# First channel layer of a mixer: product banks copied to SBUF by ScalarE instead of being added from PSUM by VectorE

## The chip, the cores and the metric

The kernel runs on one core of one Trainium2 chip. A core has five engines that work side by side, each with a queue of its own: TensorE (PE in the profile; its weight loads are PEld), VectorE (DVE), ScalarE (ACT), GpSimd (POOL) and SyncE (SP), which here only issues transfers. The metric is the device time of one execution in microseconds (us), as the median of several runs.

## The reference

Eight batches of attention with 12 heads, 448 tokens and head size 64, followed by an MLP mixer over 768 channels (token layer 448-256-448, channel layer 768-1536-768), all in float32:

```python
q_n, k_n = rmsnorm(q, g_q), rmsnorm(k, g_k)
attn = softmax(q_n @ k_n.T / 8)
x = (attn @ v) as (batch, 448, 768)
u = x + (relu(x.T @ w_tok1) @ w_tok2).T
out = u + relu(u @ w_ch1) @ w_ch2
```

## The kernel before

**Stages.** Batch b's mixing runs while the attention of batch b + 1 is computed; the last batch has no attention beside it. Batches 0 and 1 multiply the two channel layers plainly. In batches 2 to 7 both layers use a scheme with fewer products: a layer's operands are taken as blocks, 15 products (`NF9`) of sums of blocks are formed, and the results are sums of products. The sums of the weights, the "forms", are made once by POOL in batches 0 to 2 (`form`, L295), in the tiles of `raw_pool` (5 buffers), and stored in DRAM (`ws1`, `ws2`); they are placed every `FORMS_EVERY` us of a nominal clock. The sums of the data are made by VectorE and POOL as they are needed (`X1_STEPS` for layer one, in the tile `tu`; `X_STEPS` for layer two, in the slots of `hb`).

**Items.** `ch1(b, f, o)` is product f of layer one, half o of its columns; `ch2(b, f, x)` is product f of layer two, half x. Each such item is four float32 matmuls of 128x128 by 128x224 (eight records in the trace), 1.51 us of TensorE, so that a batch has 30 items of ch1 and then 30 of ch2, numbered here from 0 to 59; (4,1) means f = 4, second half.

**PSUM.** There are eight banks: four in the pool S of the attention's scores (`s_ps`, `d_ps`), two in the pool O of its values, two in the pool M (`m_ps`). A product of ch1 with o = 0, and every second product of ch2, takes a bank of S (then named `c_ps`); the others take one of M. A bank is free again when the operations that read it are done. In `ch1`, the table `C1_STEPS` says what reads it: "a" is a ScalarE copy (L989), "v" a VectorE sum and "g" a POOL sum (both L992); "P" is the bank, (m, n) a block of the hidden layer, A, B, C running sums. So most of the products are added by VectorE straight out of PSUM, 128x448 at a time, once for each o. ReLU is applied by ScalarE to a whole block (L996) when its last sum is made; `put_off` postpones this, and the data's sums, to the start of the next item.

**Attention between the items.** A pair step of attention is cut into two blocks. The first one (`first_block`) has two scores, the last values of the pair before, `row_sums` and a third score; the second one (`second_block`) has four scores and four values. `place` puts six blocks of 5.5 to 7.5 us ahead of the items 0, 9, 16, 25, 33 and 40 (`BLOCKS`): second, first, second, first, second, first. What goes with a block is issued right after it (`beside`) or spread over the items up to the next block (`between`). With a first block come, for the next pair: two squares on ScalarE (L1374, the first ahead of the block's last item, the second within the block), two sums of squares ("reduce", VectorE, L1388), then `fold` (four small ScalarE copies "half", L1396), `guess` (two small VectorE operations), three `newton` steps (POOL, four small operations each, L1418 to L1421), the sums of exponentials `group_sums` ("es", VectorE, L482, 128x896), and the denominators of the pair before (dt, rc, rd, uT on VectorE, L543 to L560). With a second block come two scales (VectorE, L403, which need the newtons), four transposes (VectorE, L418), two multiplications by g (ScalarE, L421) and four es sums. The exponentials themselves (L445) are on ScalarE.

**Order.** The order on TensorE, VectorE, ScalarE and POOL is the order in which the program issues the instructions; no scheduler moves them. An engine works through its queue in this order, and an instruction that waits holds up all that is behind it.

The lines that decide where a sum of squares stands:

```python
ahead, beside = (squares[:1], squares[3:]) if t > BIG else ([], [])
between = [item(group_sums, t, k) for k in (1, 2) if live]
...
between += roots[:1] + ends[:2] + roots[1:2]
```

`squares` is square, reduce, square, reduce for the two halves of a pair; `squares[3:]` is the second reduce, and `roots[:1]` is `fold`.

## Time and profile before

| | |
|---|---|
| median of 3 runs | 1316.96 us (1314.82 to 1317.05) |
| profiled execution | 1318.08 us, of which the span from first to last instruction is 1316.2 us |
| mean granted TensorE clock | 0.992 of full speed |
| batch 2 (mixing) begins | 426.7 us; batches 3 to 7 at 587.9, 741.7, 895.3, 1048.7 and 1196.5 us |
| VectorE sum, 128x448, one operand in PSUM (L992) | 0.61 us |
| VectorE sum, 128x896, all in SBUF (L1021, L482) | 1.08 us at its shortest, 1.17 in the mean |
| POOL sum, 128x448 (L992) and 128x896 (L1021) | 1.14 us at its shortest, and 2.09 us |
| ScalarE copy of a bank (L989), ReLU of a block (L996) | 0.53 and 0.95 us |

A span of the trace is read in three ways here: which engine waited for which, in sums; the instructions of one engine in order of time, with the idle time ahead of each and what ended it; and busy time and granted clock by stretches.

### The profile page before, as it was taken

The numbers are of one execution on the slowest core, as the hardware profiler recorded it, in microseconds if no ns is written. First come the engines' busy times: TensorE is split into PE (matmuls) and PEld (weight loads), VectorE is DVE, ScalarE is ACT, GpSimd is POOL, SyncE is SP. The second block draws the span as 40 slices with busy tenths as digits, with TensorE's granted clock in tenths as the row PEclk, the third lists the DMA queues.
The fourth block names the chain that finished last, engine by engine and source line by source line (L and its number), as shares of the span: only waits on it lengthen the run. The fifth ranks groups of instructions, "written<-read, shape, count | busy, mean of one in ns | idle before, by whom it ended". The sixth has DMA issues, their size and how long they took to land.

```text
span 1316.2 us, 19628 instructions
## 1 busy us (share of the span) xinstructions
PE 1262.6 (96%) x7048; PEld 871.8 (66%) x7048; DVE 835.9 (64%) x1280; ACT 403.5 (31%) x775; POOL 469.0 (36%) x727
## 2 busy tenths in 40 slices
PE   5999999999999997999999999999999999999996
PEld 3444444444445675696777777786876967797996
DVE  6998769654463566755768368765677557664343
ACT  6663433123320243402443044321434024300210
POOL 1300100079975785430343203450234303430242
PEclk9999999999999999999999999999999999999998
DMA  9666456898888977596567766495765965476664
GB/s 210 172 178 162 120 139 169 203 259 236 234 202 230 212 210 183 114 247 123 115 174 157 191 144 148 115 232 139 167 153 113 252 122 129 122 183 157 177 178 82
DMA packets 480272, 225.60 MB, mean 171 GB/s; under 512 B 375204, under 2 KB 441764, under 8 KB 480164
## 3 DMA queue, kind: packets, MB, share of 16 engines
q1 hardware_dynamic: 462690, 206.68, 65.2%
q0 software_dynamic: 4480, 15.73, 3.9%
q10 hardware_dynamic: 12994, 1.84, 0.9%
q8 instruction: 58, 0.95, 0.3%
q14 instruction: 50, 0.41, 0.1%
HBM read 178.36 MB, written 45.81 MB: 170 GB/s over the span
## 4 chain that ended last, share of the span: by engine, by line
PE 77%; DVE 10%; DMA 4%; SPq 3%; POOL 2%; issue 2%; ACT 2%; DVEq 0%; ACTq 0%; POOLq 0%
PE m_ps L1047 12%; PE c_ps L1047 10%; PE s_ps L441 8%; PE c_ps L979 8%; PE m_ps L979 7%; PE o_ps L514 7%; PE m_ps L862 5%; PE m_ps L1010 4%; PE m_ps L935 4%; PE m_ps L1030 4%; PE t_ps L820 2%; PE m_ps L820 2%; DVE es L482 2%; DMA qk_t<-in_k_dram 2%; DVE hb L1021 1%
## 5 line engine op out<-in xcount | busy, mean ns | idle before, releaser
L445 ACT ACTIVATE e<-s_ps 128x448 f32<-128x448 f32 x294 | 141.4, 556 | 178.9 <-PE s_ps L441 168.9
L441 PE MATMUL s_ps<-qkT 64*64 64x448 f32 x1260 | 169.0, 547 | 2.5 <-DVE r L992 1.7
L1047 PE MATMUL m_ps<-hb,unit 128*128 128x224 f32 x768 | 160.4, 364 | 9.4 <-DVE r L992 9.4
L1047 PEld LDWEIGHTS m_ps<-hb,unit 128*128 128x128 f32 x768 | 150.3, 197 | 12.5 <-DVE r L992 11.1
L295 POOL TENSOR_TENSOR raw<-raw 128x128 f32<-128x128 f32 x256 | 135.2, 549 | 45.8 <-DMA out_dram<-turned 25.5
L514 PE MATMUL o_ps<-e,v 64*64 64x448 f32 x1148 | 144.8, 539 | 0.7 <-DVE uT L560 0.4
L1047 PE MATMUL c_ps<-hb,unit 128*128 128x224 f32 x672 | 135.8, 354 | 2.6 <-ACT e L445 2.0
L1047 PEld LDWEIGHTS c_ps<-hb,unit 128*128 128x128 f32 x672 | 126.3, 190 | 9.9 <-ACT e L445 4.3
L482 DVE TENSOR_TENSOR es<-es,e 128x896 f32<-128x896 f32 x90 | 105.7, 1175 | 14.6 <-ACT e L445 9.6
L441 PEld LDWEIGHTS s_ps<-qkT 64*64 64x64 f32 x1260 | 52.6, 132 | 84.1 <-issue 57.5
L979 PE MATMUL c_ps<-tu,unit 128*128 128x224 f32 x480 | 101.5, 354 | 3.9 <-ACT e L445 3.8
L979 PE MATMUL m_ps<-tu,unit 128*128 128x224 f32 x480 | 102.1, 356 | 1.7 <-DVE hb L992 1.7
L979 PEld LDWEIGHTS m_ps<-tu,unit 128*128 128x128 f32 x480 | 89.7, 190 | 9.9 <-issue 5.6
L979 PEld LDWEIGHTS c_ps<-tu,unit 128*128 128x128 f32 x480 | 90.1, 190 | 9.2 <-ACT e L445 7.6
L514 PEld LDWEIGHTS o_ps<-e,v 64*64 64x64 f32 x1148 | 52.7, 133 | 60.5 <-issue 48.0
L992 POOL TENSOR_TENSOR hb<-hb,r 128x448 f32<-128x448 f32 x36 | 49.5, 1401 | 117.6 <-DVE r L992 80.0
L1062 POOL TENSOR_TENSOR uT<-uT,r 128x448 f32<-128x448 f32 x42 | 52.5, 1262 | 104.0 <-DVE r L1062 92.0
L403 DVE TENSOR_TENSOR qk_t<-qk_t,rs 128x896 f32<-128x896 f32 (+1 forms) x42 | 55.6, 1361 | 43.5 <-POOL rs L1421 43.5
L961 POOL TENSOR_TENSOR tu<-uT 128x448 f32<-128x448 f32 x12 | 13.7, 1139 | 194.2 <-DVE uT L867 117.2
L862 PE MATMUL m_ps<-w_sb,h 128*128 128x448 f32 x192 | 74.4, 541 | 2.9 <-DVE uT L867 2.9
L1418 POOL TENSOR_TENSOR nt<-rs 128x56 f32<-128x56 f32 (+1 forms) x57 | 17.8, 313 | 160.2 <-DVE rs L1410 158.2
L1388 DVE TENSOR_REDUCE ms<-sq 128x28 f32<-128x896 f32 (+2 forms) x44 | 47.4, 1079 | 41.4 <-ACT sq L1374 38.3
(151 smaller groups left out, 1995.5 us busy)
## 6 DMA issues: line engine op xcount, KB each, us to landing
unit<-ws SPq DMA_DIRECT2D x240, 384.0 KB, 3.9
raw<-in_moe_w_ch_dram SPq DMA_DIRECT2D x72, 256.0 KB, 3.4
v<-in_v_dram SPq DMA_DIRECT2D x96, 112.0 KB, 3.9
xs<-xt SPq DMA_DIRECT2D x56, 168.0 KB, 4.5
out_dram<-turned SPq DMA_DIRECT2D x168, 56.0 KB, 2.0
unit<-wp SPq DMA_DIRECT2D x24, 384.0 KB, 4.7
ws<-raw POOLq DMA_DIRECT2D x16, 512.0 KB, 4.9
qk_t<-in_q_dram SPq DMA_DIRECT2D x144, 56.0 KB, 3.5
```

Of the source, the lines that this page charges most:

```text
L295: nc.gpsimd.tensor_tensor(out=at[o], in0=at[x], in1=at[y], op=ALU.add if op == "+" else ALU.subtract)
L403: nc.vector.tensor_tensor(out=x, in0=x, in1=r.unsqueeze(2).to_broadcast(list(x.shape)), op=ALU.mult)
L441: nc.tensor.matmul(out=pss[i][rows_of(i, a), 0:S], lhsT=qkT[h, 1, k * D:(k + 1) * D], rhs=qkT[h, 0, :], start=True, stop=True)
L445: nc.scalar.activation(out=e[:, i, :], in_=pss[i][:, 0:S], func=AF.Exp)
L482: nc.vector.tensor_tensor(out=es[:], in0=(es if k > 1 else st["e", t, 0])[:], in1=st["e", t, k][:], op=ALU.add)
L514: nc.tensor.matmul(out=st["o", p][a * D:(a + 1) * D, 0:S], lhsT=vt[rows, k * D:(k + 1) * D], rhs=e[rows, :], **kw)
L820: nc.tensor.matmul(out=st["t1", h][jc][:, 0:HC], lhsT=w1_sb[:, c, jc * P:(jc + 1) * P], rhs=st["x", b, h][:, :, c, :], start=start and c = ...
L862: nc.tensor.matmul(out=ps[:, 0:S], lhsT=st["h1", jc][:, cc * P:(cc + 1) * P], rhs=w2_sb[:, jc].rearrange("p c r -> p (c r)"), start=(jc == ...
L935: nc.tensor.matmul(out=ps, lhsT=a[:, o + 2 * half, :], rhs=natural(half * KF + t) if wide else u[:, half * KC + t, :], start=(t == 0 and h ...
L979: nc.tensor.matmul(out=ps[:, t * HS:(t + 1) * HS], lhsT=st["w"][:, tile_at % 6, :], rhs=x[:, k, :], start=(k == 0), stop=(k == 1))
L1010: nc.tensor.matmul(out=ps, lhsT=w[:, 3 * o + t, :], rhs=u[:, half * KC + t, :], start=(half == 0 and t == 0), stop=(half == 1 and t == KC ...
L1047: nc.tensor.matmul(out=ps[:, x * HS:(x + 1) * HS], lhsT=st["w"][:, tile_at % 6, :], rhs=hb[:, X_SLOT[f], i, :], start=(i == 0), stop=(i == 3))
```

## The change

In layer one every bank is copied by ScalarE, to a block of `hb` (`C1_COPY`) or to a tile T of `raw_pool`, one for both halves; the sums are made after the second half, 128x896 at a time, between SBUF tiles, by VectorE or, in more cases than before, by POOL. A, B and C lie in slots 7, 9 and 8 of `hb`. Both layers take their banks from the pool M alone. The ReLUs are issued right after the copy of an item named in `RELU`. Layer two takes its products in another order, `SEQ`: f = 3, 9, 0, 1, 2, 4 and so on, and the slots and steps of its data's sums are changed to fit; its weights are stored in that order. Forms are placed every 12.5 us instead of 15. The second sum of squares with a first block is issued after the first es sum, in `between`, and no longer in `beside`.

```diff
-X_SLOT = (6, 7, 4, 0, 8, 5, 6, 9, 3, 2, 0, 8, 4, 1, 7)
+SEQ = (tuple(range(NF9)), (3, 9, 0, 1, 2, 4, 5, 6, 7, 8, 10, 11, 12, 13, 14))
+X_SLOT = (6, 8, 4, 0, 7, 5, 6, 9, 3, 2, 0, 7, 4, 1, 8)
 X_STEPS = {
-    ("ch1", 12, 1): (("v", 6, 1, "+", 3),), ("ch1", 13, 0): (("v", 7, 6, "+", 0),),
-    ("ch1", 13, 1): (("g", 8, 7, "+", 2),), ("ch1", 14, 0): (("g", 9, 0, "+", 1),),
-    (3, 0): (("v", 1, 1, "-", 5),), (3, 1): (("v", 6, 9, "-", 5),), (4, 1): (("g", 7, 6, "-", 4),),
-    (6, 0): (("v", 4, 7, "+", 2),), (7, 0): (("v", 0, 4, "-", 1),), (8, 0): (("g", 8, 4, "+", 3),)}
+    ("ch1", 14, 0): (("g", 9, 0, "+", 1), ("v", 6, 1, "+", 3)),
+    ("ch1", 14, 1): (("v", 8, 6, "+", 0), ("g", 7, 8, "+", 2)),
+    (3, 0): (("v", 1, 1, "-", 5),), (3, 1): (("v", 6, 9, "-", 5),), (4, 1): (("g", 8, 6, "-", 4),),
+    (6, 0): (("v", 4, 8, "+", 2),), (7, 0): (("v", 0, 4, "-", 1),), (8, 0): (("g", 7, 4, "+", 3),)}
...
-C1_STEPS = (
-    (("a", (2, 1), "P", None, None),),
-    (("v", "A", (2, 1), "-", "P"),),
...
+C1_COPY = {0: (2, 1), 2: (0, 0), 3: "B", 4: "C", 5: (0, 1), 9: (2, 0)}
+C1_STEPS = {
+    1: (("v", "A", (2, 1), "-", "T"),),
+    4: (("v", "A", "A", "+", "C"), ("v", "B", "B", "+", "A"), ("g", (0, 0), (0, 0), "+", "B")),
+    6: (("v", "B", "B", "+", "T"), ("v", "C", "C", "-", "B")),
+    7: (("v", "C", "C", "-", "T"), ("g", (0, 1), "C", "-", (0, 1))),
+    8: (("g", (2, 1), (2, 1), "-", "T"),),
+    9: (("g", (2, 0), (2, 0), "-", "A"),),
+    10: (("g", (2, 0), (2, 0), "-", "E"),),
+    11: (("g", (2, 1), (2, 1), "+", "T"), ("g", (1, 1), "C", "-", "T")),
+    12: (("v", "E", "E", "-", "T"), ("v", (2, 1), (2, 1), "+", "E")),
+    13: (("v", "E", "E", "+", "T"), ("v", (1, 0), "B", "+", "E"), ("g", (1, 1), (1, 1), "-", "E")),
+    14: (("v", (1, 0), (1, 0), "+", "T"),)}
+RELU = {("ch1", 6, 1): ((0, 0),), ("ch1", 9, 1): ((0, 1),), ("ch1", 12, 1): ((2, 0),), ("ch1", 13, 0): ((2, 1),),
+        (1, 0): ((1, 1), (1, 0))}
...
-    FORMS_EVERY = 15.0
+    FORMS_EVERY = 12.5
...
-            ahead, beside = (squares[:1], squares[3:]) if t > BIG else ([], [])
+            ahead, beside = squares[:1] if t > BIG else [], []
             between = [item(group_sums, t, k) for k in (1, 2) if live]
+            if t > BIG:
+                between[1:1] = squares[3:]
...
-        ps = m_tile() if o else s_tile("c_ps")
+        ps = m_tile()
...
-        for eng, out, a, op, c in C1_STEPS[f]:
-            if op is None:
-                nc.scalar.copy(out=at[out], in_=at[a])
-                continue
...
+        if f in C1_COPY:
+            to = at[C1_COPY[f]]
+        else:
+            if o == 0:
+                r["T"] = raw_tile()[:].rearrange("p n w -> p (n w)").bitcast(F32)[:, 0:4 * HS]
+                if f == 10:
+                    r["E"] = r["T"]
+            to = at["T"] = r["T"]
+            at["E"] = r.get("E")
+        nc.scalar.copy(out=to[:, 2 * HS * o:2 * HS * (o + 1)], in_=ps[:, 0:2 * HS])
+        relus(("ch1", f, o))
+        if o:
+            for eng, out, a, op, c in C1_STEPS.get(f, ()):
+                e = nc.gpsimd if eng == "g" else nc.vector
+                e.tensor_tensor(out=at[out], in0=at[a], in1=at[c], op=ALU.add if op == "+" else ALU.subtract)
...
-    def ch2(b, f, x):
+    def ch2(b, pos, x):
         put_off_done()
+        f = SEQ[1][pos]
         if x == 0:
-            st["m"] = s_tile("c_ps") if f % 2 else m_tile()
+            st["m"] = m_tile()
```

## The prediction

> **What bounds the kernel now.** I read the page first, then the waits by engine, then the order of time on each engine in one ordinary batch. The page:
>
> ```profile
> span 1316.2 us, 19628 instructions
> PE 1262.6 (96%) x7048; PEld 871.8 (66%) x7048; DVE 835.9 (64%) x1280; ACT 403.5 (31%) x775; POOL 469.0 (36%) x727
> ```
>
> TensorE is busy for 96% and the change removes no matmul, so only its 53.6 us of idle time and its slow clock can be won. The waits of TensorE's queue (who waited for whom: us in all, times, longest):
>
> ```profile
> PE t_ps L415 <- DVE g_t L1174: 15.1, 1, 15.1
> PE m_ps L1047 <- DVE r L992: 9.4, 5, 2.0
> PE c_ps L979 <- ACT e L445: 3.8, 3, 2.8
> ...
> PE c_ps L1047 <- ACT e L445: 2.0, 3, 0.7
> ```
>
> The first is the start of the kernel, and some 10 us lie after the last matmul; neither is touched. The other three are what the change aims at. Batches begin at 587.9, 741.7, 895.3 and 1048.7, so one takes 153.6; the batch from 426.7 takes 161.2, with POOL still at the forms (L295) until 504.9. In the batch from 587.9, TensorE in order of time (start, us, engine, line, operation, count, idle before and its releaser):
>
> ```profile
> 672.24 1.78 PE L979 MATMUL c_ps<-tu,unit 128*128 128x224 f32 x8 [0.56 <-ACT e L445]
> ...
> 680.53 4.98 PE L1047 MATMUL m_ps<-hb,unit 128*128 128x224 f32 x16 [1.98 <-DVE r L992]
> 685.35 1.68 PE L1047 MATMUL c_ps<-hb,unit 128*128 128x224 f32 x8
> ...
> 711.13 3.29 PE L1047 MATMUL c_ps<-hb,unit 128*128 128x224 f32 x16 [0.63 <-ACT cv_sb L445]
> ```
>
> Three waits, 3.17 us, and sixteen matmuls that take 4.98 where others take 3.19, because the granted clock is 0.50 from 681 to 684: 1.8 more. So **an ordinary batch has 5.0 us to win**. Everything else is hidden.
>
> **What the Trainium skill says.** "TensorE: Matmul & The Clock Gate", What's actually happening: a free-running window of 3413 ns halves the clock after idleness. The trace agrees loosely: half clock after the 1.97 us wait at 524.7, none after 2.84 at 515.6. "PSUM — Partial Sum Buffer", Engine vs sequencer instructions: ScalarE's and VectorE's queues are strict first in, first out. The trace shows ScalarE idle for 7.07 before one ReLU (683.15) with later work behind it. "SBUF — State Buffer", Who interferes with whom: a VectorE operation with two SBUF inputs and a GpSimd operation that reads SBUF exclude each other; a reduce does not. The trace agrees: an es sum that met a POOL sum took 1.83 instead of 1.08, a reduce beside POOL 1.08.
>
> **The change part by part.** An item is 1.51 us of TensorE.
>
> *Work moved, costed at nothing in itself.* Per batch: VectorE's first layer goes from 28 operations of 0.61 (17.1) to 11 of 1.08 (11.9); ScalarE's from 12 copies of 0.53 to 30 (+9.5); POOL's from 10 sums of 1.14 to 8 of 2.09 (+5.3). ReLUs and X sums keep their number. In 608.0 to 680.5 ScalarE is busy 30.3 of 72.5 and POOL 18.0, so totals fit; what counts is order. If that cover were gone, 9.5 a batch would show.
>
> *Waits that go.* In the first layer a bank is now released by a ScalarE copy, and neither layer takes banks of the scores: 0.56 and 0.63 go. The first product of layer two becomes f = 3, whose operand is ready, and its bank is freed by the copy of item (14,0): 1.98 goes. Minus 5.0 with the clock. In the batch from 426.7 the waits 1.70, 1.66, 2.84, 1.97, 0.66, 0.43 and the slow clock make 11.1; with forms placed at 12.5 they end earlier (the fifteenth is placed 35 us ahead of now), so I let all go.
>
> *New wait 1, at item 9.* With two banks, an item needs the copy of the item two before it. ScalarE's order is now: copies of (4,1) and (5,0), **fold**, copy of (5,1). Fold (four "half" copies) needs the second reduce, and the change puts that reduce behind two 896-wide sums and the first es sum. Before, the reduce ran at 630.18, well ahead:
>
> ```profile
> 634.10 0.62 DVE L992 TENSOR_TENSOR r<-r,m_ps 128x448 f32<-128x448 f32 x1 [2.82 <-PE m_ps L979]
> 634.75 0.62 DVE L992 TENSOR_TENSOR hb<-hb,r 128x448 f32<-128x448 f32 x1
> 635.29 1.08 DVE L482 TENSOR_TENSOR es<-e,cv_sb 128x896 f32<-128x896 f32 x1
> ...
> 636.16 1.01 ACT L1396 COPY half<-ms 32x56 f32<-32x56 f32 x4
> 637.20 0.53 ACT L989 COPY hb<-m_ps 128x448 f32<-128x448 f32 x1
> ```
>
> From the end of (4,1): copy 0.6, sums 1.1 + 1.1, es 1.1, reduce 1.1, fold 1.0, copy of (5,1) 0.6 = 6.6, some hand-overs 0.1. TensorE has three items, 4.5, until it needs that bank. Wait 2.2 (2.0 without hand-overs, 2.9 if POOL's sum meets the es sum).
>
> *New wait 2, at item 16.* The copies of (8,0) and (8,1) stand each behind a qkT multiplication that waits for VectorE's transposes:
>
> ```profile
> 653.83 0.67 ACT L421 ACTIVATE qkT<-qkT,g_t 128x448 f32<-128x448 f32 x1 [2.67 <-DVE qkT L418]
> 657.61 0.67 ACT L421 ACTIVATE qkT<-qkT,g_t 128x448 f32<-128x448 f32 x1 [3.11 <-DVE qkT L418]
> ```
>
> Today nothing of the mixing is behind them: items (8,0) to (9,1) are read by VectorE. With wait 1 fold ends at 640.0, the guess near 643.7, POOL's three newtons (1.4 each) at 648.1, VectorE's sums of f = 6 and 7 at 649.5; the scales (L403) then take 3.94 as today, to 653.4, the transposes and es sums follow, the second multiplication ends near 658.5 and copy (8,1) at 659.1; TensorE, 2.2 late, wants that bank at 657.3: some 1.9 with the 0.2 that (9,0) waits. Waits 1 and 2 are coupled by VectorE's chain: together 2.1 to 4.5, I take 4.1.
>
> *New wait 3, at item 25.* The same with (12,1): copy, two sums, es, reduce, fold, copy of (13,1) = 6.6 against 4.5: 2.1 (2.0 to 2.5).
>
> *New wait 4, second layer.* Item 33's block puts scales, transposes and two es sums of VectorE ahead of the read of product f = 9. Counted from the end of (12,1), VectorE's queue holds: sums 2.2, es 1.1, reduce 1.1, es 1.1; a gap to the copy of (13,1) at 6.6; sums 2.2, dt and rc 1.7, guess 0.4, X sum 1.1, sum 1.1, rd and uT 1.25, X sum 1.1: 15.5. Then POOL's X sum 2.1 and two newtons of 1.4 before the scales: 20.3, up to 22.4 where POOL and VectorE exclude each other. Scales 2.1, transposes 1.1, es 2.2, read 0.6: the bank is free at 26.3 to 28.4. TensorE, with wait 3, wants it at 24.5 (22.4 of work and 2.1). Wait 1.8 to 3.9, I take 3.0. Before, that read came at 697.72, 1.9 after its product, and cost nothing since six banks were shared.
>
> *Clock.* Each wait of about 2 us may bring half clock, 1.8; a later VectorE-bound wait then shrinks. 0 to 3.6 a batch, I take 0.9.
>
> *Forms.* Each form is three loads on SP, 19 POOL operations and two POOL stores, all moved forward past SP's unit loads and POOL's newtons. TensorE did not wait in 281 to 447, eight unit buffers cover: 0, up to +6 if SP stalls on a raw buffer.
>
> *Sum.* Three ordinary batches: 4.1 + 2.1 + 3.0 + 0.9 - 5.0 = +5.1 each, +15.3. The batch from 426.7: 10.1 - 11.1 = -1.0. The one from 1048.7 has no next pair at items 25 and 33: 4.1 - 1.5 (its only wait) = +2.6. The last, without attention: ReLU (2,1) waits for a VectorE sum before copy (13,1), +0.9. Together **+17.8** on the profiled execution's 1318.1 (span 1316.2 and 1.9 around), so 1335.9; the median of the runs is 1.1 lower: **1335**. All low ends give -2 (1315), all high ends +38 (1356).
>
> **The rivals.** (a) *ScalarE is never late*, faster: the reduce ends in time for fold. For it: VectorE is lighter by 5.2 a batch and idle at 631 to 634. Against: the chain is a queue order, 6.6 against 4.5; it decides where the chain falls below 4.5. Then only wait 4's low end, 1.8, stays: 3 x 3.2 + 9.3 + 1.5 = 20 won, 1297. (b) *Forms overrun SP*: nine forms ran back to back from 290.9 to 388.3, 10.8 each, near the 12.5; late units would add up to 6: 1341. (c) *It frees less than it says*: the S banks' waits are only 3.17 - 1.98 = 1.2 a batch, so with half the new waits the sum is near 0: 1317.
>
> **How the numbers follow.** Waits as worked out 0.63, (a) 0.20, (b) 0.09, (c) 0.08. A measurement of this kernel can tell about 0.2%, 2.6 us, from no change. Faster: 0.20 and a part of (c), 0.23; same 0.05; slower 0.72. The range runs from near (a), 1300, to the high ends, 1356; the likeliest case alone is 1320 to 1352.
>
> **What would show it.** TensorE waiting for ScalarE at L985 (m_ps) before items (6,1), (9,1), (14,1), 2 us each; ScalarE's "half" idle on the reduce at about 2 us; TensorE waiting for VectorE at the fourth product of layer two; no c_ps waits, none at that layer's first product. I am wrong if fold finds the reduce done, or if ordinary batches get shorter than 153.6.

## The result, and the profile after

The changed kernel takes 1371.6 us (median; 1367.9 to 1376.0) against 1317.0 for the kernel before on the same chip: ratio 1.042, 95% interval 1.038 to 1.045. The prediction, 1335 within 1300 to 1356, had the direction and missed the size by a factor of three. The profiled execution took 1367.9, with a span of 1366.1. The page:

```profile
span 1366.1 us, 19643 instructions
PE 1272.5 (93%) x7048; PEld 861.4 (63%) x7048; DVE 831.1 (61%) x1178; ACT 456.0 (33%) x883; POOL 520.5 (38%) x715
```

TensorE is busy 9.9 us longer and idle 40 us longer than before. The span is read batch by batch, a batch counted from its first matmul of L820 (us; the last column runs to the end of the span):

| kernel | batch 2 begins | batch 2 | 3 | 4 | 5 | 6 | 7 |
|---|---|---|---|---|---|---|---|
| before | 426.6 | 161.1 | 153.8 | 153.6 | 153.4 | 147.8 | 119.9 |
| after | 438.8 | 170.8 | 160.0 | 160.0 | 161.2 | 153.7 | 121.6 |
| more | +12.2 | +9.7 | +6.2 | +6.4 | +7.8 | +5.9 | +1.7 |

So three places are to be explained: what happens ahead of batch 2, where only the forms had been moved; batch 2; and the ordinary batch.

**The ordinary batch.** TensorE in batch 4 of the changed kernel, in order of time (start, us, engine, line, operation, count; in brackets the idle time before and its releaser):

```profile
821.77 4.81 PE L985 MATMUL m_ps<-tu,unit 128*128 128x224 f32 x24 [1.92 <-ACT hb L1000]
...
838.42 1.78 PE L985 MATMUL m_ps<-uT,unit 128*128 128x224 f32 x8 [1.40 <-ACT raw L1000]
841.67 1.78 PE L985 MATMUL m_ps<-uT,unit 128*128 128x224 f32 x8 [1.48 <-ACT raw L1000]
...
864.76 2.24 PE L985 MATMUL m_ps<-tu,unit 128*128 128x224 f32 x8 [2.07 <-ACT raw L1000]
866.79 5.98 PE L1057 MATMUL m_ps<-hb,unit 128*128 128x224 f32 x24
...
876.56 2.10 PE L512 MATMUL o_ps<-e,v 64*64 64x448 f32 x18 [1.24 <-DVE uT L558]
...
886.25 6.32 PE L1057 MATMUL m_ps<-hb,unit 128*128 128x224 f32 x32 [0.23 <-DVE uT L1072]
```

The reader sees the prediction's waits 1, 2 and 3 where they were placed and nearly as large, a wait 4 of almost nothing, and at 876 a wait for an O bank that was not foreseen. The half clock that stood behind the join of the layers now stands behind wait 3: 24 matmuls take 5.98 where 24 take 4.81 at full clock. Behind wait 1, on VectorE and then ScalarE:

```profile
819.04 1.08 DVE L1399 TENSOR_REDUCE ms<-sq 128x28 f32<-128x896 f32 x1
820.04 1.98 DVE L480 TENSOR_TENSOR es<-es,e 128x896 f32<-128x896 f32 x1
```

```profile
820.16 1.00 ACT L1407 COPY half<-ms 32x56 f32<-32x56 f32 x4 [2.77 <-DVE ms L1399]
821.18 0.53 ACT L1000 COPY hb<-m_ps 128x448 f32<-128x448 f32 x1
```

Fold idles 2.77 us on the late reduce, with the copy that frees TensorE's bank behind it: the forecast chain, to the instruction.

**Ahead of batch 2.** In the time from 390 to 440 us (columns: window, length, then busy us of PE, PEld, DVE, ACT and POOL with their counts, granted clock, DMA share, GB/s), first before, then after:

```profile
390.00:440.00 50.00, 50.00 (x147) 25.60 (x140) 16.68 (x29) 5.56 (x12) 30.25 (x74) 1.00 0.85 215
```

```profile
390.00:440.00 50.00, 42.30 (x120) 20.54 (x113) 14.93 (x25) 3.82 (x8) 24.26 (x56) 0.93 0.78 185
```

TensorE lost 7.7 us there and some clock. Why is read from ScalarE's order of time and from the waits of SP's queue (from 264 to 438.8 us) in the changed kernel:

```profile
408.90 0.95 ACT L1385 ACTIVATE sq<-qk_t 128x896 f32<-128x896 f32 x1 [16.15 <-DMA qk_t<-in_k_dram]
421.74 0.95 ACT L1385 ACTIVATE sq<-qk_t 128x896 f32<-128x896 f32 x1 [11.88 <-DMA qk_t<-in_k_dram]
```

```profile
SPq L287 <- DMA ws<-raw: 62.9, 9, 10.5
```

The first load of a form waits on SP for a raw tile that an earlier form is still storing, 62.9 us in nine waits; in the kernel before the same line (its L289) waited 34.7 us in six. The q and k loads of the next pair stand behind it in SP's queue:

```profile
400.10 0.37 SPq L287 DMA_DIRECT2D raw<-wp  x1
...
405.62 1.52 SPq L1366 DMA_DIRECT2D qk_t<-in_k_dram  x3
```

The squares wait for these loads (in the kernel before one square waits 9.2 us there, and TensorE does not wait for it), VectorE's reduce waits for the squares, and behind the reduce stand VectorE's reads of TensorE's banks:

```profile
422.72 1.09 DVE L1399 TENSOR_REDUCE ms<-sq 128x28 f32<-128x896 f32 x1 [11.22 <-ACT sq L1385]
...
426.33 0.58 DVE L1044 TENSOR_TENSOR uT<-uT,m_ps 128x448 f32<-128x448 f32 x1
```

```profile
411.56 9.29 PE L1039 MATMUL m_ps<-hb,unit 128*128 128x448 f32 x24 [1.57 <-DVE uT L1044]
426.97 11.99 PE L1039 MATMUL m_ps<-hb,unit 128*128 128x448 f32 x24 [6.13 <-DVE uT L1044]
```

The two waits are 7.7 us, and the half clock behind the second 2.7 more (11.99 against 9.29 for the same 24 matmuls). In the whole of batch 1 TensorE is busy 172.0 us instead of 166.9, with no matmul added.

### The profile page after: what moved, and what is told of

The parts are those of the page before. It is cut to its first block, busy times and chain, and to the rows that moved or that the text cites. A ratio compares the mean times of both kernels' runs of the same rounds, so it can differ in the third digit from the quotient of the medians.

```text
span 1366.1 us, 19643 instructions
## 1 busy us (share of the span) xinstructions
PE 1272.5 (93%) x7048; PEld 861.4 (63%) x7048; DVE 831.1 (61%) x1178; ACT 456.0 (33%) x883; POOL 520.5 (38%) x715
## 4 chain that ended last, share of the span: by engine, by line
PE 51%; DVE 21%; POOL 12%; DMA 4%; issue 4%; SPq 3%; ACT 3%; DVEq 0%; POOLq 0%; ACTq 0%
PE m_ps L1057 16%; PE m_ps L985 13%; POOL raw L293 7%; PE o_ps L512 5%; PE s_ps L439 4%; PE m_ps L935 4%; PE m_ps L862 4%; DVE es L480 3%; DVE hb L1005 2%; PE t_ps L820 2%; DVE qk_t L401 2%; PE m_ps L820 1%; DMA ws<-raw 1%; DVE ms L1399 1%; DVE raw L327 1%
## 5 line engine op out<-in xcount | busy, mean ns | idle before, releaser
L1057 PE MATMUL m_ps<-hb,unit 128*128 128x224 f32 x1440 | 280.4, 356 | 4.7 <-DVE uT L1072 4.7
L1057 PEld LDWEIGHTS m_ps<-hb,unit 128*128 128x128 f32 x1440 | 273.5, 192 | 14.9 <-DVE uT L1072 7.2
L985 PE MATMUL m_ps<-tu,unit 128*128 128x224 f32 x960 | 195.9, 361 | 19.3 <-ACT hb L1000 10.3
L985 PEld LDWEIGHTS m_ps<-tu,unit 128*128 128x128 f32 x960 | 182.4, 193 | 34.7 <-ACT hb L1000 12.0
L439 PE MATMUL s_ps<-qkT 64*64 64x448 f32 x1260 | 150.3, 545 | 0.8 <-ACT x L802 0.8
L293 POOL TENSOR_TENSOR raw<-raw 128x128 f32<-128x128 f32 x256 | 130.0, 528 | 40.8 <-DMA out_dram<-turned 24.5
L480 DVE TENSOR_TENSOR es<-es,e 128x896 f32<-128x896 f32 x90 | 106.8, 1187 | 12.5 <-ACT e L443 8.1
L1005 POOL TENSOR_TENSOR hb<-hb,raw 128x896 f32<-128x896 f32 x30 | 71.1, 2380 | 100.6 <-DVE raw L1005 61.6
L985 PE MATMUL m_ps<-uT,unit 128*128 128x224 f32 x480 | 96.9, 356 | 12.3 <-ACT raw L1000 12.3
L985 PEld LDWEIGHTS m_ps<-uT,unit 128*128 128x128 f32 x480 | 89.6, 190 | 19.3 <-ACT raw L1000 15.5
L1005 POOL TENSOR_TENSOR hb<-hb 128x896 f32<-128x896 f32 x18 | 45.5, 2529 | 92.5 <-DVE hb L1005 90.7
L1000 ACT COPY raw<-m_ps 128x448 f32<-128x448 f32 x108 | 56.7, 531 | 68.5 <-PE m_ps L985 66.7
L401 DVE TENSOR_TENSOR qk_t<-qk_t,rs 128x896 f32<-128x896 f32 (+1 forms) x42 | 60.4, 1475 | 27.9 <-POOL rs L1432 27.8
```

Of the source, the lines that this page charges most:

```text
L293: nc.gpsimd.tensor_tensor(out=at[o], in0=at[x], in1=at[y], op=ALU.add if op == "+" else ALU.subtract)
L401: nc.vector.tensor_tensor(out=x, in0=x, in1=r.unsqueeze(2).to_broadcast(list(x.shape)), op=ALU.mult)
L439: nc.tensor.matmul(out=pss[i][rows_of(i, a), 0:S], lhsT=qkT[h, 1, k * D:(k + 1) * D], rhs=qkT[h, 0, :], start=True, stop=True)
L480: nc.vector.tensor_tensor(out=es[:], in0=(es if k > 1 else st["e", t, 0])[:], in1=st["e", t, k][:], op=ALU.add)
L985: nc.tensor.matmul(out=ps[:, t * HS:(t + 1) * HS], lhsT=st["w"][:, tile_at % 6, :], rhs=x[:, k, :], start=(k == 0), stop=(k == 1))
L1000: nc.scalar.copy(out=to[:, 2 * HS * o:2 * HS * (o + 1)], in_=ps[:, 0:2 * HS])
```

## The experiments

**The theories.** First theory: what was not forecast is SP's queue, where loads of forms that wait for a raw tile hold up all other loads; the ordinary batch is the late reduction and the copies behind it. Rivals: POOL's forms or the tiles T in the raw pool are the limit ahead of and in batch 2; in the ordinary batch VectorE is late whatever the banks and the reduction are. Three of the four edits (forms, reduction, banks) were each taken out of the changed kernel, each of the four was put alone into the kernel before, and what remained was then tried on the sums of layer one. The changed kernel without the copies was not run. The batches of every run, from its profile:

| run | batch 2 begins | batch 2 | 3 | 4 | 5 | 6 | 7 |
|---|---|---|---|---|---|---|---|
| e1 after, forms at 15 | 427.8 | 170.6 | 160.0 | 160.0 | 160.0 | 153.8 | 121.0 |
| e2 before, forms at 12.5 | 439.6 | 165.8 | 153.7 | 152.3 | 151.2 | 147.8 | 119.7 |
| e3 after, early reduce | 443.3 | 174.7 | 160.4 | 160.4 | 160.4 | 155.3 | 120.8 |
| e4 before, layer-2 banks turned | 428.1 | 161.1 | 152.1 | 151.1 | 151.0 | 146.0 | 120.1 |
| e5 after, forms' loads on POOL | 436.2 | 169.5 | 159.9 | 160.1 | 160.0 | 153.8 | 121.0 |
| e6 before, 12.5, loads on POOL | 437.0 | 159.4 | 151.9 | 151.6 | 151.3 | 147.9 | 119.6 |
| e7 after, S banks | 438.9 | 171.7 | 160.3 | 160.4 | 160.4 | 152.6 | 119.8 |
| e8 before, M banks only | 428.1 | 163.5 | 154.0 | 154.1 | 155.9 | 150.5 | 122.0 |
| e9 copies alone, halves | 427.3 | 170.8 | 155.4 | 154.4 | 153.9 | 148.6 | 119.6 |
| e10 copies alone | 429.2 | 180.9 | 160.1 | 158.3 | 157.1 | 151.0 | 119.4 |
| e11 before, layer 2 in M | 425.6 | 165.9 | 153.7 | 152.8 | 153.9 | 146.2 | 120.0 |
| e12 before, late reduce | 429.0 | 166.4 | 154.0 | 154.0 | 154.0 | 149.0 | 120.2 |
| e13 e9 with a pool for T | 459.8 | 194.7 | 166.3 | 167.3 | 167.5 | 163.9 | 126.9 |
| e15 after, halves | 444.5 | 172.9 | 160.4 | 159.1 | 159.0 | 153.1 | 120.6 |
| e16 e13, layer-2 banks turned | 461.6 | 193.6 | 157.9 | 159.6 | 158.0 | 154.6 | 119.9 |
| e17 after, S banks and halves | 442.0 | 173.5 | 157.3 | 157.1 | 157.2 | 150.3 | 119.8 |
| e18 e9 with T in slot 6 | 425.9 | 169.2 | 155.1 | 153.7 | 153.0 | 148.5 | 119.9 |
| e19 e18, layer-2 banks turned | 425.1 | 169.0 | 157.9 | 156.2 | 154.0 | 148.2 | 120.1 |

### The forms: e1, e2, e5, e6

```diff
-    FORMS_EVERY = 12.5
+    FORMS_EVERY = 15.0        # e1, in the changed kernel; e2 is the reverse edit in the kernel before
```

> The changed kernel with FORMS_EVERY put back from 12.5 to 15.0 and nothing else undone. Theory (SP's in-order queue: the loads of a form wait there for a raw tile, and the next pair's q and k loads, the x loads and the sends of the output wait behind them): the wait of ScalarE's square for qk_t (16.15 and 11.88 us) falls below 3, the 6.13 us of PE behind the bank reads of L1044 go, batch 2 starts near 427 instead of 438.8 and lasts about 163 instead of 171.0; sum 18 to 22 us, time about 1351. Rival (POOL's own work or the T tiles in the raw pool are what binds): the forms that are no longer done in batch 1 fall into batch 2, which grows by 5 or more, and the time stays above 1362. Batches 3 to 6 keep their 6 to 8 us over the kernel before under both.

Measured: 1359.2 us, ratio to before 1.036 (1.033 to 1.039). Batch 2 begins at 427.8: eleven of the twelve us are back. Batch 2 stayed at 170.6, so the theory held for the part ahead of batch 2 and failed for batch 2 itself, which lasts as long with forms at 15 as at 12.5. One square still waits 10.7 us for its loads, where the theory had less than 3, but TensorE does not wait for it.

> The kernel before with FORMS_EVERY 12.5 instead of 15.0 and nothing else changed. Theory (SP's queue alone, without the new layer-1 code): batch 1 ends 8 to 14 us later, batch 2 is up to 8 longer, batches 3 to 7 stay within 0.5 each; time 1317 + 12 to 20, about 1333. Rival A (it takes T in the raw pool to hold up the forms' tiles): under +4, time below 1321. Rival B (the faster forms do help where they are): time below 1317.

Measured: 1331.6, ratio 1.012 (1.009 to 1.015), batch 2 at 439.6 and 4.7 us longer: the theory's numbers, and no layer 1 with copies is needed for them. Not foreseen: batches 4 and 5 are 1.3 and 2.2 shorter than before.

The next two send the three raw loads of a form through POOL's queue, which itself works through the forms in order:

```diff
-            nc.sync.dma_start(out=flat[:, 0:6 * P].rearrange("p (m n) -> p m n", m=2), in_=rows(0, 2))
+            nc.gpsimd.dma_start(out=flat[:, 0:6 * P].rearrange("p (m n) -> p m n", m=2), in_=rows(0, 2))
...
```

> The changed kernel, forms at 12.5, with the three raw loads of a form issued on POOL's queue instead of SP's. Theory (it is the queue of SP in which the loads that wait for a raw tile hold up the q, k and x loads and the sends): batch 2 starts at 428 or earlier instead of 438.8 (gain of 9 to 12), the waits for qk_t (16.15 and 11.88 us on ScalarE) fall below 4, and batch 2 loses its waits for x and the sends (5 to 8 us of 170.8); batches 3 to 7 as they were; time about 1355. Rival (POOL's adds at the closer spacing hold up VectorE or the T tiles, whichever queue issues the loads): batch 2 starts at 435 or later, time above 1366.

> The kernel before with forms at 12.5 and the three raw loads of a form issued on POOL's queue. Theory (SP's queue): the 12 us that the closer forms cost up to batch 2's start and the 4.7 us in batch 2 go, the 1.5 and 2.2 us that they gain in batches 4 and 5 stay; time 1310 to 1316, at or below the kernel before. Rival (POOL's adds at the closer spacing are what costs): time above 1325.

Measured: e5 1364.9, ratio 1.037 (1.032 to 1.042); e6 1323.3, ratio 1.006 (1.004 to 1.008). Both are half a miss. Batch 2 begins at 436.2 in e5 and at 437.0 in e6: by this sign, 435 or later, the rival in e5's expectation was right. The stretch that had lost 7.7 us in the changed kernel shows that its reason was not; here it is in e5:

```profile
390.00:440.00 50.00, 50.00 (x176) 24.37 (x168) 19.02 (x31) 7.22 (x16) 41.81 (x88) 1.00 0.97 239
```

TensorE is never idle there, at full clock, with forms at 12.5 and more POOL work than before (41.81 against 30.25). So at the end of batch 1 it is not POOL's work that holds TensorE up, and with the loads off SP's queue the loss there is gone. What e5 gained there it lost at the start of batch 1, in TensorE's order of time:

```profile
271.52 1.94 PE L827 MATMUL t_ps<-x,w_sb 64*128 64x384 f32 x4 [8.73 <-DMA x<-xs]
273.39 6.05 PE L820 MATMUL t_ps<-x,w_sb 128*128 128x384 f32 x12
```

TensorE now waits 8.7 us for the x loads, which every batch begins with (8.3 in e6). The trace of e5 shows POOL issue a form's two stores and the next form's three loads from 258.06 to 261.86, while SP issues the x loads from 258.57 to 265.35; in the changed kernel SP issues them from 256.35 to 260.68, and a form's loads only after them. That this crowding is what made them late was not tested apart. In e6 the 4.7 us of batch 2 are gone (159.4), as the theory had it; most of the twelve ahead of batch 2 are not, for they went over to the x loads.

### The ordinary batch, one edit at a time: e3, e7, e8, e12, e10

```diff
-            ahead, beside = squares[:1] if t > BIG else [], []
+            ahead, beside = (squares[:1], squares[3:]) if t > BIG else ([], [])
...
-            if t > BIG:
-                between[1:1] = squares[3:]
```

> The changed kernel with the second reduction of the squares put back to its place beside the first block. Theory (the late reduction holds up the fold's copies, and ScalarE stands behind them while PE waits for a layer-1 bank): waits 1 and 3 of an ordinary batch (1.92 and 2.07 us, with about 0.9 of half clock) go, the qkT wait (1.40 + 1.48) and the uT waits stay; batches 3 to 5 shorter by 3 to 5 each, 12 to 20 in all, time about 1356. Rival (VectorE's queue is what is late; the reduction early delays its other work as much): under 4 us in all, time above 1367.

Measured: 1375.5, ratio 1.045 (1.043 to 1.048): a clear miss. TensorE's waits in batch 4 of e3 (us in all, times, longest):

```profile
PE o_ps L512 <- DVE uT L558: 4.6, 2, 2.3
PE m_ps L983 <- ACT raw L998: 3.9, 3, 1.5
PE m_ps L1055 <- DVE uT L1070: 1.7, 2, 1.0
```

Wait 1 went and wait 3 fell to 1.05 (no wait for hb is left, none of 2 us for raw), nearly as the theory said. In their place TensorE reaches the attention blocks earlier and waits for an O bank, 4.6 us instead of 1.2. The rival was right: VectorE is next.

```diff
-        ps = m_tile()
+        ps = m_tile() if o else s_tile("c_ps")
...
-            st["m"] = m_tile()
+            st["m"] = s_tile("c_ps") if pos % 2 else m_tile()
```

> The changed kernel with the banks of S given back to both layers (half 0 of a layer-1 product, every second layer-2 product), the copies, the late reduction and the forms at 12.5 kept. Theory (what PE waits for in an ordinary batch is a ScalarE copy that is late by one item; with two pools in turn a bank is asked for again four items later instead of two, or sooner served): waits 1 to 3 (1.92, 1.40 + 1.48, 2.07 us) go and with them 4 to 6 us of batches 3 to 5 each; time about 1345. Rival (the scores, which use S, take the wait over, or VectorE's uT is next to be late as it was when the reduction went back): batches shorter by under 2 each, waits for s_ps of 1 to 3 us in their place; time above 1360.

Measured: 1363.3, ratio 1.035 (1.030 to 1.040), and the ordinary batch 160.4: the rival again. TensorE in batch 4 of e7:

```profile
830.41 0.74 PE L512 MATMUL o_ps<-cv_sb,v 64*64 64x448 f32 x2 [2.27 <-DVE uT L558]
...
830.96 3.99 PE L512 MATMUL o_ps<-e,v 64*64 64x448 f32 x20
...
874.18 0.59 PE L439 MATMUL s_ps<-qkT 64*64 64x448 f32 x2 [3.32 <-ACT cv_sb L443]
```

No copy is waited for in layer 1 any more, and the batch is as long as ever. VectorE ahead of that O bank shows why:

```profile
817.26 2.22 DVE L1005 TENSOR_TENSOR hb<-hb 128x896 f32<-128x896 f32 x2 [6.71 <-ACT hb L1000]
819.39 1.08 DVE L480 TENSOR_TENSOR es<-cv_sb,e 128x896 f32<-128x896 f32 x1
820.39 1.08 DVE L1399 TENSOR_REDUCE ms<-sq 128x28 f32<-128x896 f32 x1
821.39 1.98 DVE L480 TENSOR_TENSOR es<-es,e 128x896 f32<-128x896 f32 x1
...
829.06 0.64 DVE L555 STREAM_TRANSPOSE rd<-rc 128x448 f32<-128x448 f32 x1
829.73 0.62 DVE L558 TENSOR_TENSOR uT<-o_ps,rd 128x448 f32<-128x448 f32 x1
```

VectorE idles 6.71 us, because a sum of 128x896 can start only when the second half of a product has been copied, and then works 13 us without a gap until uT frees the bank. It has less to do in a batch than before (100.4 us against 102.1) and does it in lumps. The other wait shown, 3.32 us of the scores for ScalarE, is there in e10 and e9 below as well (4.6 and 3.2 in batch 4).

> The kernel before with all products of both layers in the two banks of M, its PSUM adds, its early reduction and forms at 15 kept. Theory (with adds read from PSUM VectorE's queue of 102 us a batch frees the banks late): waits for m_ps on VectorE of 6 to 15 us a batch, time 1350 to 1400, so that the copies are what makes the single pool bearable. Rival (the two banks of M are enough whoever reads them): within 5 us of 1317, and then the copies are not needed.

> The kernel before with the second reduction of the squares put between the items, as in the changed kernel, and nothing else. Theory (alone it moves 1.08 us of VectorE past the sums of the group and delays fold and Newton by about 3 us, where VectorE waits for rs on POOL 8.4 us a batch): 0 to 3 us a batch longer, time 1317 to 1330. Rival (it takes VectorE's work off the place where the block's O bank is late, and helps): 1 us a batch shorter, time 1305 to 1315.

```diff
# e8, in the kernel before
-        ps = m_tile() if o else s_tile("c_ps")
+        ps = m_tile()
...
-            st["m"] = s_tile("c_ps") if f % 2 else m_tile()
+            st["m"] = m_tile()
```

```diff
# e12, in the kernel before
-            ahead, beside = (squares[:1], squares[3:]) if t > BIG else ([], [])
+            ahead, beside = squares[:1] if t > BIG else [], []
...
+            if t > BIG:
+                between[1:1] = squares[3:]
```

Measured: e8 1323.9, ratio 1.006 (1.005 to 1.008), a miss for both theories: 8 us lost, not 35 and not 5. e12 1320.6, ratio 1.005 (1.004 to 1.007), 154.0 in an ordinary batch, as its theory had it. Alone, neither edit is dear.

> The copies and SBUF sums alone: the changed kernel with the banks of S, the early reduction and forms at 15 of the kernel before. Theory (the copies with whole sums make VectorE late whatever the banks and the reduction): batches 3 to 5 at 159 to 161 with waits of o_ps on uT of 3 us or more in each; batch 2 starts near 427 and lasts 167 to 171; time about 1352. Rival (it takes the three edits of layer 1 together to lose; each alone is harmless): batches at 153 to 155, time below 1330.

e10 is the changed kernel with the S banks of e7, the reduction of e3 and the forms of e1 together, so that only the copies, their sums and the order of products remain. Measured: 1349.9, ratio 1.026 (1.022 to 1.029). The copies alone carry more than half of the loss. By their ratios, taken of 1315 us, the four single edits cost 34 (copies), 8 (M banks), 7 (late reduce) and 15 (forms), 64 in all, and 55 together in the changed kernel. Batches 3 to 5 took 160.1, 158.3 and 157.1; the batch 2 of its profiled execution, the slowest of its four, is long.

### VectorE's lumps: e9, e15, e17

```diff
-        if o:
-            for eng, out, a, op, c in C1_STEPS.get(f, ()):
-                e = nc.gpsimd if eng == "g" else nc.vector
-                e.tensor_tensor(out=at[out], in0=at[a], in1=at[c], op=ALU.add if op == "+" else ALU.subtract)
+        half = lambda t: t[:, 2 * HS * o:2 * HS * (o + 1)]
+        for eng, out, a, op, c in C1_STEPS.get(f, ()):
+            e = nc.gpsimd if eng == "g" else nc.vector
+            e.tensor_tensor(out=half(at[out]), in0=half(at[a]), in1=half(at[c]), op=ALU.add if op == "+" else ALU.subtract)
```

> The copies alone (banks of S, early reduction and forms at 15 as in the kernel before), and the SBUF sums of layer 1 done in halves of 128x448, each right after its own copy, instead of 128x896 once a product. Theory (VectorE is late in lumps: it idles until the second half is copied, then has 13 us of sums, denominators and uT on end when the block wants its O bank): the waits o_ps on uT (3.2 us a batch with the S banks) and the half clock behind them go, batches 3 to 5 at 153 to 156; 10 us or more below the copies alone with whole sums. Rival (it is the amount of VectorE's and POOL's work, not when it comes: halves cost more in all): batches at 160 or longer, as long as with whole sums.

Measured: 1334.4, ratio 1.015 (1.012 to 1.019), 15 us below e10 with the same copies, banks, reduction and forms: batches 3 to 5 at 155.4, 154.4 and 153.9. VectorE's busy time in batch 4 is 101.7 against 102.2 in e10, so it is when the work comes and not how much. The place of the batch that was shown of e7, first in e10, then in e9:

```profile
829.70 1.01 PE L512 MATMUL o_ps<-cv_sb,v 64*64 64x448 f32 x2 [2.27 <-DVE uT L558]
...
830.52 3.60 PE L512 MATMUL o_ps<-e,v 64*64 64x448 f32 x20
```

```profile
811.38 0.59 PE L512 MATMUL o_ps<-cv_sb,v 64*64 64x448 f32 x2 [0.64 <-DVE uT L558]
...
811.82 2.41 PE L512 MATMUL o_ps<-e,v 64*64 64x448 f32 x20
```

The wait fell from 2.27 to 0.64, and with it the half clock: 20 matmuls in 2.41 instead of 3.60. VectorE ahead of it, again e10 and then e9:

```profile
816.55 2.22 DVE L1003 TENSOR_TENSOR hb<-hb 128x896 f32<-128x896 f32 x2 [2.90 <-ACT hb L998]
...
819.80 2.85 DVE L480 TENSOR_TENSOR es<-es,e 128x896 f32<-128x896 f32 x1
```

```profile
799.86 1.28 DVE L1003 TENSOR_TENSOR hb<-hb 128x448 f32<-128x448 f32 x2 [2.71 <-ACT hb L998]
...
802.18 1.91 DVE L480 TENSOR_TENSOR es<-es,e 128x896 f32<-128x896 f32 x1
```

From these sums to uT VectorE works without a gap, 13.1 us in e10 and 11.5 in e9. Of the 1.6 us between them 0.9 is the sum whose first half was made before (1.28 instead of 2.22) and 0.9 the es sum, beside which POOL made a sum of 128x896 in e10 and of 128x448 in e9 (2.80 and 1.85 us); later sums take 0.2 back. So the halves help twice, for the edit cuts POOL's sums as well; no run cut VectorE's alone.

> The changed kernel, with its two M banks, late reduction and forms at 12.5, and only the sums of layer 1 done in halves of 128x448. Theory (lumps on VectorE are behind what cannot be won back in an ordinary batch whichever bank or reduction is put right): the 160.0 us of batches 3 to 5 fall to 154 to 158; the waits for ScalarE's copies behind fold and the qkT multiplications partly stay, 3 to 5 us a batch; time 1371 minus 8 to 25. Rival (with two banks the copies' place behind fold and qkT decides, the lumps only with the S banks): batches stay within 1 us of 160.0, time above 1365.

> The changed kernel (late reduction, forms at 12.5) with both the banks of S in both layers and the sums of layer 1 in halves. Each of the two alone left the ordinary batch at 159 to 160.4 us. Theory (two limits lie at nearly the same place: with two banks PE waits for copies behind fold and qkT, with the S banks for VectorE's lump; only both together free PE): batches 3 to 5 at 153 to 156, time 1340 to 1350. Rival (it was the early reduction or the forms at 15 that brought the batches to 154 in the run with copies and halves): batches at 158 or longer, time above 1358.

Measured: e15, halves in the changed kernel with nothing else, 1373.0, ratio 1.042 (1.038 to 1.046), batches at 159.0 to 160.4: nothing, the rival of its expectation. e17, halves and S banks, 1355.5, ratio 1.028 (1.026 to 1.031), batches at 157.1 to 157.3: between its two theories. So in the changed kernel two limits stand nearly at the same place, PE waiting for a copy behind fold or qkT, and PE waiting for a bank behind VectorE's lump. Removing either one uncovers the other at once (e7 160.4, e15 159.0 to 160.4); removing both gives 2.7 to 4 us. The last 3 us, to the 154 of e9, come from the early reduction and the forms at 15 together; which of the two was not separated.

### Batch 2: e18, e13

Batch 2 is 7.5 us longer than an ordinary batch before and 10.8 after, so 3 of its 9.7 us are its own and the rest is the ordinary loss. In e5 and e9 ScalarE's copies there wait for a raw tile that a form holds, here in e9:

```profile
486.23 0.53 ACT L998 COPY raw<-c_ps 128x448 f32<-128x448 f32 x1 [4.05 <-POOL raw L297]
...
491.95 0.53 ACT L998 COPY raw<-c_ps 128x448 f32<-128x448 f32 x1 [3.78 <-DMA ws<-raw]
```

```diff
# e13, on top of e9
-    raw_pool = pool("raw_pool", 5)
+    raw_pool = pool("raw_pool", 4)
+    t_pool = pool("t_pool", 2)
...
-    turn_pool = pool("turn_pool", 4)
+    turn_pool = pool("turn_pool", 3)
```

> The copies with sums in halves (as in the run before with halves), and the tiles T taken from a pool of their own with two buffers; for room the raw pool has 4 buffers instead of 5 and the pool of turned outputs 3 instead of 4. Theory (batch 2's surplus of 10 us over the kernel before is ScalarE's copy waiting for a raw tile that a form of the weights still holds, 3 to 9 us at a time): batch 2 falls from 170.8 to 158 to 164 although the forms have a buffer less, the other batches stay at 154; time 1334 minus 7 to 12. Rival (it is the forms themselves, through POOL and the ports that VectorE shares with it, that slow batch 2's layer 1): batch 2 stays above 168, time 1330 or more.

Measured: 1447.2, ratio 1.098 (1.094 to 1.102). It answers nothing on batch 2: with four raw tiles and three output tiles other waits rose, and T with two buffers is too few (19.6 us of scores waiting for copies into T in the whole run). The next one took the raw tiles away from T without touching a pool:

```diff
-                r["T"] = raw_tile()[:].rearrange("p n w -> p (n w)").bitcast(F32)[:, 0:4 * HS]
+                r["T"] = h(6) if f < 10 else raw_tile()[:].rearrange("p n w -> p (n w)").bitcast(F32)[:, 0:4 * HS]
```

> The copies with S banks and sums in halves (early reduction, forms at 15), and the tiles T of the products 1, 6, 7 and 8 put into slot 6 of hb, which layer 1 does not use until its last product, instead of a raw tile; all pools as they were. Theory (in batch 2 a T in the raw pool waits for a form's tile, and a form's loads on SP's queue wait for a T): the waits of the copies for raw (4.05 and 3.78 us) and of the square for qk_t (6.16 and 9.37 us) shrink, batch 2 falls from 170.8 to 161 to 166, the others change by less than 1.5; time 1334 minus 5 to 10. Rival (batch 2 is long by POOL's forms and their ports; or the single slot makes ScalarE wait for the readers of T): batch 2 above 169, or batches 3 to 5 longer by 2.

Measured: 1333.1, ratio 1.012 (1.009 to 1.014), the same as e9 within the intervals, and batch 2 at 169.2. The two waits for raw tiles are gone and 1.6 us with them: the rival. What is left is in VectorE's and ScalarE's order of time in e18:

```profile
515.24 5.88 DVE L1003 TENSOR_TENSOR raw<-raw 128x448 f32<-128x448 f32 x1 [11.80 <-POOL hb L1003]
```

```profile
522.93 0.95 ACT L1383 ACTIVATE sq<-qk_t 128x896 f32<-128x896 f32 x1 [10.01 <-DVE ms L1397]
523.78 0.96 ACT L443 ACTIVATE e<-s_ps 128x448 f32<-128x448 f32 x2
```

VectorE's sum into E must wait until POOL has read E for (2, 0), and POOL's sum stands behind a form in POOL's queue. VectorE's reduce waits behind that sum, the square behind the reduce, the exponentials behind the square, and TensorE 7.1 us for the bank that they read. In batch 2 POOL's forms are thus on the path through the new sums, as one rival said. It was read in e18's trace; no run took it away.

### Versions that could be faster: e4, e11, e16, e19

```diff
-            st["m"] = s_tile("c_ps") if f % 2 else m_tile()
+            st["m"] = m_tile() if f % 2 else s_tile("c_ps")
```

> The kernel before with the parity of the second layer's banks turned round: the products of even f take a bank of S, those of odd f one of M. Theory (the wait of 2.0 us at the join of the layers is one for an S bank that ScalarE copies out late; the first product of layer 2 takes the other pool): that wait and its half clock (1.8 us) go in the batches that have it, 4 to 15 us in all, time 1302 to 1313. Rival (the wait only goes over to the next item with a bank of the other pool, or to the scores that use S after layer 2): within 2 us of 1317, with a new wait of 1 to 3 us in each batch.

Measured: 1311.3, ratio 0.997 (0.995 to 0.998) over 17 runs of it. This one line in the kernel before is the best of all versions: the wait of 2.0 us at the join goes, in batch 5 the scores behind layer 2 wait 1.9 us in its place, and yet batches 3 to 5 are 1.7 to 2.5 shorter, because TensorE is busy 149.1 us in batch 5 instead of 150.6: the half clock went.

```diff
# e11, in the kernel before
-        ps = m_tile() if o else s_tile("c_ps")
+        ps = s_tile("c_ps") if o else m_tile()
...
-            st["m"] = s_tile("c_ps") if f % 2 else m_tile()
+            st["m"] = m_tile()
```

> The kernel before with the halves of layer 1 turned round (half 0 in M, half 1 in S) and all of layer 2 in M. Theory (layer 2 alone is content with two banks: 0.6 us of waits a batch where both layers had M only; and its first product no longer asks for the bank that layer 1 used last): the wait of 2.0 us at the join, its half clock and the 1.9 us of the scores behind layer 2's S banks go, batches 3 to 5 at 150 to 151, time 1300 to 1310. Rival (a wait of the same size comes back for the scores behind layer 1's half 1, or in layer 2's own copies): 1312 or more.

> The copies with sums in halves and T in a pool of its own, and layer 2's banks turned round as in the run of the kernel before that gained by it. Theory (the join's wait and its half clock are the same thing there): 3 to 8 us below the same kernel with the old parity, 1315 to 1323. Rival (with the copies the join has no wait any more, c_ps on exponentials 0.7 us and scores on ScalarE 3.2 us are what is left): within 2 us of it.

> The kernel of the run before this one, with layer 2's banks turned round (even products in S, odd ones in M). Theory (the join's wait is the same there as in the kernel before, which gained 4 us by it): 2 to 6 us below that run. Rival (with the copies the join has no wait, what is left are scores that wait for ScalarE, 3.2 us a batch): within 2 us of it.

Measured: e11 1326.1, ratio 1.009 (1.006 to 1.012), a miss; the waits come back as c_ps on exponentials and m_ps on layer 2's own sums, 11 us each in the whole run. e16 is e13 with the turned banks, 1406.0, ratio 1.067 (1.064 to 1.071): 41 us below e13, but with e13's shortage of tiles the two tell little. e19 is e18 with them, 1331.0, ratio 1.009 (1.007 to 1.012): 2.2 us below e18, on the border of its two expectations and within their intervals. In batch 4 of e18 TensorE has no wait at the join that could go, and in e19 new waits of 1.9 us for an O bank and 2.0 for VectorE come up. No version with the copies comes below the kernel before.

## Why the prediction was wrong, point by point

In the profiled execution 49.9 us were lost where 17.8 were forecast. Of the 32.1 that were missed 12.2 lie ahead of batch 2, 10.7 in batch 2, 5.1 in the three ordinary batches, 3.3 in batch 6 and 0.8 in the last.

**Forms: this step failed most.** "0, up to +6 if SP stalls on a raw buffer" measured +12.2 ahead of batch 2 (e1 gives back 11, e2 costs 13 alone). The prediction named the very mechanism, counted the three loads on SP, and then asked only whether the unit loads are late: "eight unit buffers cover". The unit loads were covered; the q and k loads of the next pair, which have no such cover, were not costed. The count under rival (b) was off too: from 290.9 to 388.3 the trace of the kernel before has eight forms back to back, 12.2 us each, and not nine of 10.8. That leaves next to no room within 12.5.

**The batch from 426.7.** Forecast -1.0, measured +9.7. New waits and clock were forecast at 10.1. Waits 1 to 3 measured 7.5 (6.2 forecast), wait 4 0.2 (3.0 forecast), and 2.3 came that no step had (1.24 for an O bank, 1.01 for a later sum of layer two); that these add up to 10.0 is chance. "I let all go" of 11.1 gave only the 9.3 of waits, while the clock got worse (TensorE busy 154.8 instead of 151.9). Another 5.9 came as waits for x loads (3.0) and for the token layer's reads (L867, 2.9). These are the closer forms again: e2 has both (3.6 and 5.3), e1 neither. Yet e1's batch 2 is as long, because its copies are waited for longer there (13.4 us instead of 7.5).

**Ordinary batches.** Forecast +5.1, measured +6.2 to +7.8. Waits 1, 2 and 3 were forecast at 4.1 + 2.1 and measured 1.92 + 2.88 + 2.07 = 6.9. Wait 4, forecast 3.0, measured 0.23. VectorE's read freed the bank at 886.2, 28.3 us after the end of (12,1), as forecast (26.3 to 28.4); but TensorE, which the forecast had there at 24.5, came at 28.1, held up by then 1.2 us at the O bank and 1.6 by the half clock. The prediction had said that such a wait then shrinks. The layer's uT sums cost 1.2 in all, that 0.23 among them. Of the 5.0 that were to be won only the waits of 3.0 went: TensorE is busy 150.6 us in batch 4 before and after, for the half clock went from the join to wait 3. -3.0 + 6.9 + 1.2 (O bank) + 1.2 (uT sums) is 6.3, and 6.4 was measured.

**Work moved, "costed at nothing in itself".** The sums that were moved came out near the forecast, the totals did not. In batch 4 ScalarE's busy time grew by 8.7 us (9.5 forecast), VectorE's fell by 1.8 (5.2 forecast) and POOL's rose by 9.7 (5.3 forecast), because work that was not moved took longer: POOL's newtons 16.2 us instead of 12.0, VectorE's scales 9.1 instead of 8.1. What was not costed either is that a whole sum starts a half later than a half sum and delays all that is queued behind it: e10 against e9, 15 us, with POOL's share in it. The forecast gave the loss to the late reduction and the two banks; e3 and e7 take away the waits that these make, and win nothing in an ordinary batch. So the waits were right as places, and wrong as the price of the change.

**Batch 6.** Forecast +2.6, measured +5.9: waits 1 and 2 were 1.9 and 1.4 (3.3 against 4.1), and the O bank, which no step had, 3.1. The last batch, +0.9, measured +1.7, of which 0.8 is the wait that was named.

**Rivals and range.** (b), forms overrun SP, had the queue right, but unit loads as what is late, and put at 6 what cost 12. (a) is refuted by waits 1 to 3, and so is (c), which halved them, though less was freed than the 5.0 claimed. Added up as given, with the clock's 3.6 in batch 2 too, the high ends come to +42 and not +38; the result lies beyond both.

## What to carry to other kernels

A wait in the trace shows who is late first, not what it would cost to remove: where two in-order queues are late at nearly the same moment, each repair alone measures as nothing, so look at the next releaser of the same stretch before a gain is claimed. When an operation is made larger to save instructions, cost the time until its last input is there and everything queued behind it, not its busy time. When loads are placed earlier on a shared queue, ask what each of them waits for and list every other load behind it with its own slack, not the best-buffered one.

## What the runs showed of the hardware

**Half clock after short waits.** The same join of layers in the kernel before and in e2, TensorE in order of time:

```profile
987.53 4.98 PE L1047 MATMUL m_ps<-hb,unit 128*128 128x224 f32 x16 [1.97 <-DVE r L992]
```

```profile
1003.26 3.29 PE L1047 MATMUL m_ps<-hb,unit 128*128 128x224 f32 x16 [1.81 <-DVE r L992]
```

After 1.97 us idle the 16 matmuls took 4.98, after 1.81 they took 3.29. It is why e2's batch 5 is 2.2 us shorter with nearly the same waits. The Trainium skill, "TensorE: Matmul & The Clock Gate", What's actually happening, has a window of activity that runs free of the waits, and puts half clock after an idle window of about 3.4 us. A window that runs free of the waits agrees with the traces: 2.07 us brought half clock in batch 4 of the changed kernel and 1.92 did not, nor did 2.84 in batch 2 of the kernel before (518.4), so the length alone does not decide. The 3.4 us do not agree: here 1.97 us idle was enough. That the phase of the window decides is likely, but no run changed the phase alone.

**VectorE beside POOL.** Two scales of 128x896 (L401) took 4.90 us in the changed kernel where POOL's sums ran beside them (831.3), and 2.09 at another place of the same batch (789.3). One 128x448 sum in e18 took 5.88 instead of 0.62 while six POOL sums ran back to back, and ended 0.5 us after the last of them. The Trainium skill, "SBUF — State Buffer", Who interferes with whom, has a VectorE operation with two SBUF inputs and a GpSimd operation that reads SBUF exclude each other; the durations agree, and the last one looks as if VectorE had waited for all six and not for one. Moving VectorE's sums from PSUM to SBUF puts more of its work under that rule.
